# The last two row blocks of a gated mix as one: first feed-forward layer by seven quarter products

## Chip, cores and metric

The kernel runs on one core of a Trainium2 chip. The metric is device time in microseconds, as the median of several executions. The profile is one execution seen by the hardware profiler, with its own time. TensorE (PE) multiplies, VectorE (DVE) and GpSimd (POOL) do elementwise work, ScalarE (ACT) does copies and functions, and SyncE (SP) issues most DMAs.

## The reference

```python
x = A_x                                   # 1 x 2048 x 512, all float32
g = _sigmoid((x * gate_w).sum(-1, keepdims=True))
a = _A_ref(x, A_wqkv, A_w_phi, A_wo)      # linear attention, 32 heads of 16
b = _B_ref(x, B_w1, B_b1, B_w2)           # mish(x @ w1 + b1) @ w2, 512 -> 1376 -> 512
return g * a + (1 - g) * b
```

In the attention q and k go through a 16x16 matrix per head; the feature map of each is the softmax of the result beside the softmax of its negative. Then `kv = phi_k^T v`, `z` is the sum of `phi_k` over all rows, and the output is `(phi_q kv) / (phi_q z)`, times `wo`.

## The kernel before, in words

**Precision.** Each matmul operand is split in a high part (ScalarE's copy to fp32r) and a low part (VectorE or GpSimd: the value minus the high part). A product is three groups of matmuls: high by high, high by low, low by high. The moving side is 512 wide, so 128 of the contraction against 512 columns is one matmul; every matmul goes through the helper `mm` (L130), every ScalarE instruction through `act` (L157), so the profile tells them apart by tile names.

**Stages.** P fuses the 16x16 matrices into the weights of q and k. A0 to A7 take 256 rows of x each: they make q, k and v (tiles `proj`), write q to DRAM (`pqd`), and collect `kv` (tile `kvp`) and `z`. In A1 to A7, q and k come out of seven products of half operands instead of eight (steps `s1` to `s7`, with the sums `bc`, `ca`, `qa`). B0 to B3 take 512 rows each: the feed-forward layers, softmax of q, the numerator, the output projection, the gate and the output. W steps load and split w1, w2 and wo.

**A row block B.** The first layer has 11 units of 128 columns (`up0` to `up10`). `up` makes 12 matmuls, `w1` against `xbh` and `xbl`, in one bank; `mi` is Mish with the bias; `h` and `l` split the result; the second layer (`dn`, tile `down`) adds, for each of four row tiles a to d, three matmuls per unit into a bank of its own. Unit 0 holds the last 96 columns of the first 736 and the gate; its low part is packed in spare rows (`ha`, `hb`, `ph`, `pi`, `pc`), so it takes two matmuls per row tile and one short piece (`dc`). For attention, `lq` loads q, `mx`, `mn`, `d0`, `d1`, `E`, `S` make both softmaxes, `T`, `D`, `m`, `de`, `rd`, `sc`, `es` the denominator and scaling, `tr`, `st`, `ld` turn the features by way of DRAM (`eTd`, `eT`), `nu` is the numerator (32 short matmuls, tile `num`), `oh` and `ol` split it, `wo` is the output projection (12 matmuls). `ag`, `fi` and `so` scale it with the gate, add the second layer and store.

**Order.** Each engine runs its instructions in the order of the table `ORDER`. A line names a stage; a word is a step of it, and `B1:` ahead of a step means another stage. A step's last letter v or g says VectorE or GpSimd. `@` gives buffer or bank numbers; `^` makes a GpSimd step wait for the VectorE step written ahead of it. Words of different engines that stand side by side need not run at the same time.

**PSUM and SBUF.** Of eight banks three have the tag `a` (first layer, num, wo), four `dn` (second layer) and one `kv`. `w1` in both parts lies at a fixed place (the arena, 11264 floats per partition); x's two parts and the gather tiles lie in the pool.

Of the kernel before, what the change touches and what calls it, by code (L numbers as in the profile page):

```python
# [91 lines left out]
def tile_gated_mix(ctx: ExitStack, tc: tile.TileContext, xT, wv, wkT, wqT, bd, w1a, w1b, b1, w2a, w2b, wo, out):  # L92
# [29 lines left out]
    nc.alloc_sbuf_tensor("arena", [P, sum(FIXED.values())], F32)
    top = nc.sbuf_base
    for tag, n in list(FIXED.items()):
        top -= 4 * n
        for part, o in (("h", 0), ("l", 2 * n)):
            FIXED[tag + part] = {dt: nc.alloc_sbuf_tensor_at(tag + part + x, [P, n // 2], dt, offset=top + o) for dt, x in ((F32R, "r"), (F32, "f"))}

# [905 lines left out]
```

## Time and profile before

| | |
|---|---|
| median of 3 runs | 439.56 us (439.36 to 439.75) |
| profiled execution | 439.43 us |
| its span | 437.7 us, 7246 instructions |
| TensorE busy | 432.8 us, 2835 matmuls |
| VectorE, ScalarE, GpSimd busy | 319.9, 231.4, 182.3 us |
| DMA | 55.14 MB, mean 126 GB/s |
| chain that ended last | by line: proj 28%, up 28%, down 27%, wo 10%, num 2% |

In the profile an instruction's line ends with the number of instructions, then busy time and mean length, and behind the bar the idle time of its engine ahead of it with what ended it. A row of the chain is start, length and what ran. A matmul's own length overlaps with the next one's, so a run of matmuls is read by start and end of the whole piece.

### The profile page before, as it was taken

To read this page: it belongs to the slowest core of one execution; us is meant where nothing else is said; L and a number is where in the kernel's file an instruction comes from. 1 tells how busy PE (TensorE), PEld (TensorE's weight loads), DVE (VectorE), ACT (ScalarE), POOL (GpSimd) and SP (SyncE) were. 2 spreads that over 40 slices of the span, in tenths; PEclk is the share of its full clock that TensorE was granted. 3 is DMA by queue.
4 is the path that set the end of the run, shared out by engine and by line. 5 is a ranking of instruction groups with operands and counts; after the bars stand their busy time and mean duration, and the time that the engine had idled before them with its cause. 6 is when DMAs were issued, how large, how long until landed. Compare 5 with 4: busy or idle time off the path is not lost.

```text
span 437.7 us, 7246 instructions
## 1 busy us (share of the span) xinstructions
PE 432.8 (99%) x2835; PEld 352.0 (80%) x2835; DVE 319.9 (73%) x441; ACT 231.4 (53%) x317; POOL 182.3 (42%) x147
## 2 busy tenths in 40 slices
PE   8999999999999999999999999999999999999996
PEld 7888888888888888887878887878888778888775
DVE  3996799789988989998784896676776537557212
ACT  3775446538444958673633826638646166262321
POOL 4438748858568013565034452131442500631210
PEclk9999999999999999999999999999999999999999
DMA  7612284676982423463302244321614410034303
GB/s 272 234 73 75 119 191 117 171 172 153 262 233 89 143 77 96 145 214 120 114 12 96 96 155 160 120 74 54 211 49 168 135 35 25 24 108 173 121 32 120
DMA packets 30041, 55.14 MB, mean 126 GB/s; under 512 B 5364, under 2 KB 15348, under 8 KB 30008
## 3 DMA queue, kind: packets, MB, share of 16 engines
q1 hardware_dynamic: 27960, 48.26, 32.8%
q0 software_dynamic: 1904, 6.17, 7.4%
q8 instruction: 22, 0.36, 0.3%
q10 hardware_dynamic: 144, 0.26, 0.2%
q14 instruction: 11, 0.09, 0.1%
HBM read 32.26 MB, written 22.03 MB: 124 GB/s over the span
## 4 chain that ended last, share of the span: by engine, by line
PE 99%; DVE 0%; DVEq 0%; issue 0%
PE proj L130 28%; PE up L130 28%; PE down L130 27%; PE wo L130 10%; PE num L130 2%; PE kvp L130 2%; PE fuse L130 1%; PE warm L130 1%; PE z L130 0%; DVE io L886 0%; PE kvT L654 0%; DVEq L1030 0%; DVE ones L190 0%
## 5 line engine op out<-in xcount | busy, mean ns | idle before, releaser
L705 POOL TENSOR_TENSOR l<-act,h 128x512 fp32r<-128x512 f32 x28 | 37.7, 1346 | 117.9 <-ACT h L157 37.5
L157 ACT ACTIVATE act<-up,cst 128x512 f32<-128x512 f32 x44 | 30.1, 687 | 54.8 <-PE up L130 47.3
L157 ACT ACT_TABLE_LOAD x34 | 43.6, 1283 | 5.6 <-PE up L130 5.0
L317 DVE TENSOR_REDUCE Sm<-E 128x64 f32<-128x1024 f32 x32 | 38.7, 1208 | 6.6 <-ACT E L157 6.6
L130 PE MATMUL wo<-woh,ohl 128*128 128x512 f32 x128 | 41.4, 389 | 0.0
L157 ACT ACTIVATE h<-act 128x512 fp32r<-128x512 f32 (+1 forms) x48 | 30.0, 629 | 18.9 <-PE down L130 10.8
L130 PE MATMUL down<-w2ah,h 128*128 128x512 f32 x96 | 38.0, 396 | 0.0
L157 ACT ACTIVATE E<-E 128x1024 f32<-128x1024 f32 x32 | 33.4, 1056 | 8.4 <-DVE E L311 4.7
L130 PE MATMUL down<-w2al,h 128*128 128x512 f32 x96 | 37.4, 390 | 0.0
L130 PE MATMUL down<-w2bh,h 128*128 128x512 f32 (+1 forms) x81 | 31.5, 389 | 0.0
L130 PE MATMUL down<-w2bl,h 128*128 128x512 f32 (+1 forms) x81 | 31.3, 387 | 0.0
L130 PE MATMUL down<-w2bh,l 128*128 128x512 f32 (+1 forms) x81 | 31.3, 386 | 0.0
L130 PE MATMUL down<-w2ah,l 128*128 128x512 f32 x80 | 31.1, 389 | 0.0
L130 PEld LDWEIGHTS wo<-woh,ohl 128*128 128x128 f32 x128 | 24.0, 188 | 5.0
L836 DVE STREAM_TRANSPOSE E<-E 128x1024 f32<-128x1024 f32 x16 | 19.9, 1243 | 10.3 <-POOL E L333 10.0
L130 PE MATMUL up<-xbh,w1ahr 128*128 128x512 f32 x96 | 25.9, 392 | 0.0
L130 PE MATMUL up<-xbh,w1alr 128*128 128x512 f32 x96 | 25.7, 389 | 0.0
L130 PE MATMUL up<-xbl,w1ahr 128*128 128x512 f32 x96 | 25.7, 389 | 0.0
L886 DVE SCALAR_TENSOR_TENSOR io<-down,cst,io 128x512 f32<-128x512 f32 (+1 forms) x17 | 11.7, 705 | 18.7 <-ACT io L157 9.3
L130 PE MATMUL wo<-wol,ohl 128*128 128x512 f32 x64 | 24.9, 389 | 0.0
L130 PEld LDWEIGHTS down<-w2ah,h 128*128 128x128 f32 x96 | 18.0, 188 | 5.6 <-issue 1.2
L796 DVE TENSOR_REDUCE Dn<-T 128x64 f32<-128x1024 f32 x16 | 19.3, 1208 | 4.3 <-POOL T L792 4.0
(197 smaller groups left out, 1062.6 us busy)
## 6 DMA issues: line engine op xcount, KB each, us to landing
eTd<-E SPq DMA_DIRECT2D x16, 512.0 KB, 2.6
eT<-eTd SPq DMA_DIRECT2D x64, 128.0 KB, 2.7
xraw<-in_xT_dram SPq DMA_DIRECT2D x15, 512.0 KB, 4.1
zd<-E POOLq DMA_DIRECT2D x10, 512.0 KB, 5.4
pqd<-qs SPq DMA_DIRECT2D x16, 256.0 KB, 3.7
pq<-pqd SPq DMA_DIRECT2D x16, 256.0 KB, 2.9
out_dram<-io SPq DMA_DIRECT2D x10, 256.0 KB, 2.0
raw<-in_w2a_dram SPq DMA_DIRECT2D x3, 512.0 KB, 4.3
```

What stands on the lines that cost most here:

```text
L130: return pin(nc.tensor.matmul(*a, **k))
L157: return pin(A_.activation(out_, in_, fn, **k))
L317: pin(V.tensor_reduce(d["S"], hv(d["E"][:, :]), axis=AX.X, op=ALU.add))
L705: on_(e)(e.tensor_sub(U[i]["l"], U[i]["a"], f32(U[i]["h"])))
L796: pin(V.tensor_reduce(d["D"], hv(d["T"][:, :]), axis=AX.X, op=ALU.add))
L836: at(key, f"tr{t}", lambda d=d: pin(V.transpose(d["E"][:, :], d["E"][:, :])))
L886: pin(V.scalar_tensor_tensor(io[t][:, sl], dn[t][:, sl], og_sb[:, i % 8 : i % 8 + 1], io[t][:, sl], op0=ALU.mult, op1=ALU.add))
```

## The change

B2 and B3 become one block of 1024 rows, S1 (B0 and B1 stay). Its first layer is computed in pairs of units. With x in four quarters (512 rows by half of the 512 features) and the weights of two units in four quarters (half of the features by 128 columns), a pair takes seven products of a quarter by a quarter instead of eight, six matmuls each:

- x's quarters and their sums, eight operands in high and low parts, lie over `w1`'s place and x's old place, once B1 is done with them. Quarters are loaded anew from DRAM (`x11` and so on, 18 DMAs of 256 KB), and five sums (`t3`, `t2`, `t1`, `ta`, `t4`) are made.
- Weights are loaded anew for each pair (`la`, `lb`: 6 DMAs, 1 MB) and summed (`sa`: two, `sb`: three operations of 128x256), then split (`wah`, `wal`, `wbh`, `wbl`).
- A pair's products: `s1` opens a bank, `bc` copies it to a second bank, `s2` ends the first; `s7` goes to the `kv` bank, which `cm` copies out; `s6` and `s5` go on in the second bank; `ca` adds the second bank and `cm`'s copy into a third, `s4` ends that; `qa` updates the copy, `s3` ends the second bank. `ma` to `md` are Mish for two units and two row halves.
- Activations of the second row half go to DRAM and come back (`sp`, `al`, ten units of 256 KB each way), and their second layer (`en`) comes after that of the first half.
- The single unit's split weights are stored and loaded again for the second half (`wst`, `wl_1`).
- The gathers of S1 all use the one tile `eT`; `tt` is the place of the pair's weights.
- `ORDER` is new from its first line on, for all stages.

The diff, cut to its core:

```diff
-SLOTS = "01201010213"
+SLOTS = "01201010123"
 ORDER = """
-    P0| lk0 fk0@01 lx0@0 xh0 xl0g kh01 kl01 lk2 fk2@23 kh00 p0a0@0 kl00 p0a1@1 p0b1 lx1 xh1 lk1 xl1g^ fk1 kh11 kh10 lk3 fk3 kl10 lx2 xh2 kh21 lq3 kl11 p0c1 kl21 p1a1
+    P0| lk0 lx0@0 xh0 lx2 fk0@01 kh00 xh2 kh01 p0a0@0 kl00 kl01 p0a1@1 lk1 xl0g^ fk1 kr00 kr01 xl2v p0b0 p0c0 lq0 kh10 lq1 kh11 kl11 fq0@23 lx1 xh1 xl1g fq1 qh01 kl10
...
+    B1| S1:XL11g dn9c es3v tr3 mi10@1 h10@3 S1:d01v@2 S1:T0v@0 S1:d11v S1:E1 st3 S1:xt1 mi4@0 h4@5 S1:mx2@1 l4g^@4 dn9ad S1:D0@1 ol0 wo0 wo1@0 dn1b S1:S1@1 S1:la0
+    S1| sa0g^ B0:so1 B1:ag0@1 B1:dn1d B1:ld2 B1:ld3 B1:nu1@1 B1:oh1@01 T1v@1 B1:dc D1@0 B1:dn4b m1 de1 B1:l10g@0 B1:dn10d t1v mn2@1 XL21v B1:dn10a d12g@0 x22 lq4@1 XHt1
+    S1| B1:ol1 B1:wo2 XH22 XHt3 B0:so3 B1:wo3@2 XL22v B1:dn4d xt4 XLt1v d02g lb0@0 sb0v B1:h3@6 B1:l3v@7 B1:dn3da E2 T2v@0 wah0 B1:dn10c wal0v XHt2 XLt2v wl_0@0 wh_0@1
+    S1| wo_0v tag^ wst B1:ag2@3 B1:ag3@2 B1:fi3 B1:so3 B1:dn3c B1:dn4c B1:fi2 u0@1 mu0@1 gr0@0 gs0 B1:so2 hb0@2 s10@2 B1:dn4a mx4@0 ha0@5 B1:dn3b bc0@1 t4v B1:dn10b s20
+    S1| XLt3v XHt4 s70 s60 la1 XLt4g^ ph0 pi0 dn0c@2 ma0@4 dn0a@0 h01@6 S0@0 dn0b@3 m0 B1:fi0 B1:ag1@2 de0 B1:fi1 cm0@7 ca0@2 l01g@3 dn1b wbh0@3 wbl0g s40 rd0 sc0 sa1g
+    S1| s50 lb1@0 dn1d@1 mb0@0 rd1 sc1 pc0 dn0d h02@4 wah1 qa0 md0 s30 l02v@1 dn2b wal1v B1:so0 sb1g^ es1v sp2 tr1 mc0@5 sp1 dn1c st1 ge0 gg0 s11@0 bc1@2 s71 s61 wbh1@3
...
+    S1| sc5 dn9cad mn6@1 d16v@3 md3 dn9b cm4@7 ca4@2 s44 mb4@2 mx6@1 h010@5 sp8 d06v al4@0 dn8d al1@6 s54 l010v@3 dn10ba m4 h12@2 dn10cd wo3@0 l12g^@5 qa4 md4 sp10 wo2
...
-    FIXED = {"w1a": NFA * 1024, "w1b": NFB * 1024}
...
+    AREA = 17408
...
+    for tag, o, *sizes in ((("w1a", 0, NFA * 512, NFA * 512), ("w1b", NFA * 1024, NFB * 512, NFB * 512), ("xbh", 11264, 2048), ("xbl", 13312, 2048), ("tt", 15360, 2048), ("wa", 15360, 1024, 1024),
+                            ("wb", 14336, 512, 512)) + tuple((f"xo{i}", 2048 * i, 1024, 1024) for i in range(7))):
+        fixed(tag, o, *sizes)
...
+    XTAG = {"11": 0, "21": 1, "t3": 2, "t2": 3, "t1": 4, "22": 5, "t4": 6, "12": 4}
+    PAIRS = ((0, 1), (2, 3), (4, 6), (7, 8), (9, 10))
...
+            def prod(bank, n, b, o, start, stop):
+                m = 0
+                for wi, xi in ((0, 0), (1, 0), (0, 1)):
+                    for k in range(2):
+                        c, t = b * 256 + k * P, wv_(n, wi)
+                        if (n, b) == ("b", 2):
+                            c, t = wi * 256 + k * P, w["c"]
+                        mm(ps[bank], t[:, c : c + P], xv(o, xi)[:, k, :], start=(start and m == 0), stop=(stop and m == 5), skip_group_check=True)
+                        m += 1
...
+            def bc():
+                ps["q0"] = psum("up", "a")
+                act(ps["q0"], ps["k0"])
+
+            def ca():
+                ps["k1"] = psum("up", "a")
+                pin(V.tensor_add(ps["k1"], ps["q0"], U[1, j]["a"]))
+
+            def cm():
+                U[1, j] = {"a": k2("act", "hl")}
+                act(U[1, j]["a"], ps["m7"])
+
+            def qa():
+                pin(V.tensor_add(U[1, j]["a"], ps["q0"], U[1, j]["a"]))
...
+            at(key, f"s2{p}", lambda: prod("k0", "a", 1, "21", False, True))
+            at(key, f"s6{p}", lambda: prod("q0", "a", 3, "t2", False, False))
...
+            at(key, f"s5{p}", lambda: prod("q0", "b", 1, "t1", False, False))
+            at(key, f"s4{p}", lambda: prod("k1", "b", 0, "t4", False, True))
...
+            at(key, f"s3{p}", lambda: prod("q0", "b", 2, "22", False, True))
...
-    for b in range(NB):
+    for b in range(2):
         b_ops(b)
+    sb_ops(1)
```

The remaining steps of S1 (softmax, numerator, output projection, gate, output, second layer) do for 1024 rows what B2 and B3 did for 512 each.

More of the change, by code (lines that the diff above doesn't have):

```diff
@@ L119, in tile_gated_mix, with fixed @@
     ENG = (("v", V), ("g", G_))
-    FIXED = {"w1a": NFA * 1024, "w1b": NFB * 1024}
[L122 to L127, printed above, removed]
+    FIXED = {}
+    AREA = 17408
+    nc.alloc_sbuf_tensor("arena", [P, AREA], F32)
+    base = nc.sbuf_base - 4 * AREA
+    def fixed(tag, o, *sizes):
+        n = sum(sizes)
+        for part, q, size in [("", 0, n)] + [(p, i * sizes[0], m) for i, (p, m) in enumerate(zip("hl", sizes)) if len(sizes) > 1]:
+            FIXED[tag + part] = {dt: nc.alloc_sbuf_tensor_at(tag + part + x, [P, size], dt, offset=base + 4 * (o + q)) for dt, x in ((F32R, "r"), (F32, "f"))}
+    for tag, o, *sizes in ((("w1a", 0, NFA * 512, NFA * 512), ("w1b", NFA * 1024, NFB * 512, NFB * 512), ("xbh", 11264, 2048), ("xbl", 13312, 2048), ("tt", 15360, 2048), ("wa", 15360, 1024, 1024),
+                            ("wb", 14336, 512, 512)) + tuple((f"xo{i}", 2048 * i, 1024, 1024) for i in range(7))):
+        fixed(tag, o, *sizes)
     def mm(*a, **k):
@@ L308, in dd @@
             E = hv(d["E"][:, a * 512 : (a + 1) * 512])
-            note = on_(e) if key[0] == "B" else pin
+            note = on_(e) if key[0] in "BS" else pin
             if (a == 0) != negative:
@@ L321, in feat_ops @@
         for a in range(2):
-            if key[0] == "B":
+            if key[0] in "BS":
                 for x, e in ENG:
@@ L710, in down_mm @@
                 dn[t] = psum("down", "dn")
-            if part[1] == 512:
-                left[t] -= 1
-            sl = slice(*part)
-            mm(dn[t][:, sl], a, w[:, sl], start=(n == 3 * NF), stop=(n == 1), skip_group_check=True)
+            left[t] -= 1
+            mm(dn[t], a, w, start=(n == 3 * NF), stop=(n == 1), skip_group_check=True)
         def down(i, t):
-            parts = ((0, 512),)
-            if b == NB - 1 and len(left) == 4 and sum(left.values()) == 3:
-                ends.append(t)
-                parts = ((0, 256), (256, 512))
-            for part in parts:
-                for a, x in (("h", 0), ("h", 1), ("l", 0)) if i else (("h", 0), ("i", 1)):
-                    down_mm(t, U[i][a][:, t * P : (t + 1) * P], w2_tile(UNITS[i], x), part)
-        ends = []
-        def cols(t):
-            return (slice(0, 256), slice(256, 512)) if t in ends else (slice(None),)
+            for a, x in (("h", 0), ("h", 1), ("l", 0)) if i else (("h", 0), ("i", 1)):
+                down_mm(t, U[i][a][:, t * P : (t + 1) * P], w2_tile(UNITS[i], x))
         def ha(x):
@@ L896, in b_ops, with save, rows @@
         x_ops(b)
+    XTAG = {"11": 0, "21": 1, "t3": 2, "t2": 3, "t1": 4, "22": 5, "t4": 6, "12": 4}
+    PAIRS = ((0, 1), (2, 3), (4, 6), (7, 8), (9, 10))
+    actd, wsplit = {}, {}
+    def save(k, parts):
+        n = parts[0].shape[1]
+        wsplit[k] = tc.dram_tile([P * len(parts), n], F32, name=f"ws{k}")
+        for j, t in enumerate(parts):
+            pin(Sy.dma_start(wsplit[k][j * P : (j + 1) * P, :], f32(t)))
+    def rows(c):
+        return slice((c % 2) * SC, (c % 2) * SC + SC)
```

419 lines of the change are left out of this document (370 added, 49 removed).

## The prediction

> **What bounds the kernel now.** I read the page first, then TensorE's waits, then the chain of waits that ended last, then the groups of instructions, the stretches of the last two row blocks, and the timeline of VectorE and GpSimd beside each other. The page:
>
> ```profile
> span 437.7 us, 7246 instructions
> ...
> PE 432.8 (99%) x2835; PEld 352.0 (80%) x2835; DVE 319.9 (73%) x441; ACT 231.4 (53%) x317; POOL 182.3 (42%) x147
> ...
> PEclk9999999999999999999999999999999999999999
> ...
> PE 99%; DVE 0%; DVEq 0%; issue 0%
> ```
>
> TensorE is busy 99% of the span, at the full granted clock, and it alone is the chain. TensorE's waits have one line, ahead of the first matmul:
>
> ```profile
> PE warm L130 <- DVE ones L190: 1.1, 1, 1.1
> ```
>
> A busy TensorE can still be waiting inside, since ends are modelled, so I look at its pace. The chain, in order of time:
>
> ```profile
> 5.38 1.60 PE fuse L130 x64
> ...
> 7.05 1.19 PE proj L130 x3
> 8.25 1.09 PE fuse L130 x64
> 9.34 6.36 PE proj L130 x27
> ...
> 282.44 2.72 PE up L130 x12
> ...
> 331.78 10.20 PE down L130 x45
> ...
> 345.38 1.02 PE num L130 x32
> ...
> 434.02 0.03 issue
> 434.05 0.48 DVE io L886
> ```
>
> Twelve up matmuls take 2.72 us and 45 down matmuls 10.20 us: 227 ns each, in both rows. The start is looser: 30 proj matmuls at that pace are 6.80 us and took 7.55, and the first 64 fuse matmuls took 0.51 us longer than the second 64. So about 1.3 us of waiting sits at the start and almost none behind it. The matmuls end at 434.05; 3.65 us of eviction, output and end follow. The profiled execution took 439.43 us (1.73 around the span), 0.13 under the median of 439.56.
>
> **TensorE's share of the change.** Now the first layer of two blocks is 2 x 11 units x 12 matmuls = 264. Afterwards ten units go in five pairs, each seven quarter products of 6 matmuls, and the eleventh stays at 12 per block: 5 x 7 x 6 + 24 = 234. Second layer, attention, output projection, and the final matmuls in halves keep their numbers. So 30 matmuls go. The price of one is not the mean in its group,
>
> ```profile
> L130 PE MATMUL up<-xbh,w1ahr 128*128 128x512 f32 x96 | 25.9, 392 | 0.0
> ```
>
> since 392 ns is how long one is in the array while the next already runs (that would give 11.8 us); it is the pace: 30 x 227 ns = **6.80 us**. On the other side nothing is added for TensorE to do, so with no new wait the profiled time is 439.43 - 6.80 = 432.6 us. Whatever else the change costs, it costs as waits in a TensorE queue that today has none.
>
> **What the other engines get.** Rows for the pieces:
>
> ```profile
> L157 ACT ACT_TABLE_LOAD x34 | 43.6, 1283 | 5.6 <-PE up L130 5.0
> L157 ACT ACTIVATE act<-up,cst 128x512 f32<-128x512 f32 x44 | 30.1, 687 | 54.8 <-PE up L130 47.3 <-PE down L130 6.4 <-DVE l L705 0.8
> L157 ACT ACTIVATE h<-act 128x512 fp32r<-128x512 f32 x40 | 25.2, 630 | 18.8 <-PE down L130 10.8 <-POOL l L705 5.6 <-DVE lc L741 1.1
> L157 ACT ACTIVATE xbh<-xraw 128x1024 fp32r<-128x1024 f32 x8 | 8.3, 1053 | 3.8 <-PE up L130 3.3 <-DMA xraw<-in_xT_dram 0.4
> ...
> L157 ACT ACTIVATE wkh<-fuse 128x256 fp32r<-128x256 f32 x2 | 0.8, 383 | 5.7 <-PE fuse L130 5.7
> ```
>
> ```profile
> L420 DVE TENSOR_TENSOR proj<-proj,qs 128x512 f32<-128x512 f32 x7 | 4.9, 697 | 1.4 <-ACT qs L157 0.8 <-PE proj L130 0.5
> ...
> L552 DVE TENSOR_TENSOR w2al<-raw,w2ah 128x1024 fp32r<-128x1024 f32 x2 | 2.4, 1210 | 0.0
> ...
> L382 DVE TENSOR_TENSOR w1blr<-sraw,w2bl 128x512 fp32r<-128x512 f32 x3 | 2.1, 687 | 0.1
> L376 DVE TENSOR_TENSOR sraw<-xraw,sraw 128x256 f32<-128x256 f32 x4 | 1.7, 422 | 0.1
> ```
>
> ```profile
> L705 POOL TENSOR_TENSOR l<-act,h 128x512 fp32r<-128x512 f32 x28 | 37.7, 1346 | 117.9 <-ACT h L157 37.5 <-DVE h L741 26.3 <-PE down L130 24.8
> ...
> L376 POOL TENSOR_TENSOR sraw<-xraw,sraw 128x256 f32<-128x256 f32 x10 | 7.6, 763 | 0.4
> ...
> L552 POOL TENSOR_TENSOR w2al<-raw,w2ah 128x1024 fp32r<-128x1024 f32 x1 | 2.4, 2402 | 4.7 <-DVE w1alr L552 4.7
> ```
>
> - ScalarE: x's high parts go from four of 128x1024 to eight (+4.2 us); per pair the weights' high parts (1053 + 630 + 383) and two copies of a bank (about 0.63 each): 3.3 us, five times 16.6; 0.6 for the single unit. Together 21.4 us. Counted in the written order, the changes between Exp and Mish go from 35 to 33, so table loads stay.
> - VectorE: two additions into a bank or tile per pair (10 x 0.70), x's sums and low parts by the order's suffix (+4 net of 128x1024, 4.8), weights' sums (6 + 3 of 128x256, 3.8), low parts (5 x 1.21 and 0.69): 22.4 us.
> - GpSimd: +5 net of 128x1024 (12.0), weights' sums (4 + 12 of 128x256, 12.2), low parts of the second half (5 x 2.11): 34.8 us.
>
> The stretches from the first matmuls of block B2 to the last matmul, with TensorE, weight loads, VectorE, ScalarE, GpSimd, clock, DMA share and GB/s:
>
> ```profile
> 0.00:20.00 20.00, 18.76 (x314) 15.75 (x315) 12.15 (x24) 12.10 (x22) 9.83 (x17) 1.00 0.71 252
> 230.50:282.50 52.00, 52.00 (x257) 42.45 (x256) 36.56 (x52) 27.76 (x34) 17.91 (x13) 1.00 0.38 132
> 282.50:354.00 71.50, 71.50 (x371) 57.48 (x370) 46.63 (x68) 39.92 (x51) 25.32 (x17) 1.00 0.33 111
> 354.00:434.00 80.00, 80.00 (x440) 63.95 (x438) 38.95 (x60) 31.78 (x45) 17.37 (x11) 1.00 0.22 76
> ```
>
> In these 203.5 us VectorE is busy 122, ScalarE 99 and GpSimd 61. With the additions, and every other step on the engine it has now: 145, 121 and 95. (The new order moves some steps between VectorE and GpSimd; their sum, 240 of 407 us, is what I hold to.) No engine is full on average. DMA gets 14.3 MB more (x's quarters 2.6, weights 5.2, the single unit's weights 1.3, ten activations out and back 5.2), 70 GB/s over these stretches, on 76 to 132; the first 20 us moved 252. SP's queue gets some 65 issues. The price of a fetch of 256 KB, from issue to landing, has this row:
>
> ```profile
> pq<-pqd SPq DMA_DIRECT2D x16, 256.0 KB, 2.9
> ```
>
> With ScalarE's copy and GpSimd's difference a fetched unit is ready 2.9 + 0.63 + 1.35 = 4.9 us after its issue. For seven of the ten fetches the order has 2 to 21 us of TensorE's work between fetch and first use; units 3, 5 and 9 are fetched right ahead of it, and are hidden only if SP gets there early, as it does now for B3's last gather, which stands right ahead of its num matmuls. SP waits for the fetch's buffer, and behind it stand x's last quarter, output stores and the attention gathers, for which the last single unit and the num matmuls wait. I take nothing for these; one of the three exposed would give up to 4.9 us, 439.0 in all.
>
> **Where it can pinch.** The start is reordered too: I count its 1.3 us as unchanged, between all of it gone and twice it. At the end nothing changes in kind. The opening of the merged block is the dense place, and here a resource counts that the page has no column for. VectorE and GpSimd beside each other:
>
> ```profile
> 186.74 1.28 POOL L705 TENSOR_TENSOR l<-act,h 128x512 fp32r<-128x512 f32 x1 [1.36 <-ACT h L157]
> ```
>
> ```profile
> 186.90 1.17 DVE L808 TENSOR_TENSOR Dn<-Dn 128x32 f32<-128x32 f32 x1
> ...
> 206.60 0.19 DVE L808 TENSOR_TENSOR Dn<-Dn 128x32 f32<-128x32 f32 x1
> ```
>
> VectorE's small addition at 186.90 took 1.17 us; the same operation at 206.60, with GpSimd idle, took 0.19. The slow one ended at 188.07, just behind GpSimd's 188.02: it had waited for GpSimd's operation. So operations with two SBUF inputs on these two engines go one at a time. Count both engines' from B1's ninth unit to the first product of the second pair. TensorE has 32 x 3 + 4 x 2 down matmuls, eight products, four output projections, two units of the plain first layer, two sets of num matmuls and one short piece: 53.3 us. VectorE has 15 of 128x1024 (18.2), nine half as wide (6.2), three of 128x256 (1.3) and ten small ones (0.2 each): 27.7. GpSimd has 5 of 128x1024 (12.0), ten half as wide (13.5) and eight of a quarter (6.1): 31.6. Together 59.3, that is 6.0 more than TensorE's work. The 11.8 us ahead of it hold 8.3, so 3.5 can be done early; and about 3.5 of the 6.0 (a weight sum, a scaling) is not needed by that product. So the wait is between 0 and 2.5 us; I take 1.0. If all 6.0 came through, the time would be 438.6.
>
> The hand-offs inside a pair are the other place: a bank is copied between its first and second product, a sum is made in a fresh bank, and a tile is updated before the last product. An addition takes 0.70 us. The least work between its producer and its user in the written order is 1.13 us (five matmuls, pair 0, ahead of its last product) and 1.36 (six, pairs 1, 3 and 4). So 0.4 to 0.6 us is left for semaphores and for whatever VectorE has ahead; behind the waiting addition stand softmax steps and the next addition. One VectorE operation too many (0.69 to 1.21) costs 0.1 to 0.8. I take 0.5 for all five pairs.
>
> Sum: 439.43 - 6.80 + 1.0 + 0.5 = **434.1 us**.
>
> **The rivals.**
> 1. *The shared ports bind the opening.* For it: the 59.3 against 53.3. Against it: VectorE's and GpSimd's steps can run early. All 6.0 paid, with the 0.5: 439.1; half: 436.1. The Trainium skill's page "SBUF — State Buffer", section "Who interferes with whom", says that these engines share one port pair as an exclusive lock, held for a whole instruction; the row at 186.90 agrees.
> 2. *Every pair waits (slower).* The sum's bank can be the one that Mish is still reading. If ScalarE is in Exp then, the product waits for a table load, Mish and the addition: 1.28 + 0.69 + 0.70 = 2.7 us, five times 13.4, giving 446.0. It decides at 1.6 us per pair, (440.4 - 432.6) / 5. Against it: between the bank's last product and its next use lie 4.8 us or more of other matmuls in the three pairs that reuse it at once.
> 3. *Data late at the opening.* Behind B1's last up matmul SP issues x's quarters (1.05 MB) and weights (0.52) ahead of the second half's gathers (1.05), and these feed the num matmuls. At 252 GB/s they take 10.4 us; TensorE has 10.9 us (eight down groups and two output projections) until then. With the 2.9 us from issue to landing on top they are 2.4 us late: 0 to 2.4 us more than the forecast, to 436.5. By the Trainium skill's "TensorE: Matmul & The Clock Gate", "Part 1", a wait over about 3.4 us would also halve the clock for a while; no row here shows such a wait.
> 4. *The change does not deliver:* the order of all stages is new, and a few tenths in each of ten places give back the 6.8. Nothing in the profile speaks for it but that there is no slack: 439 to 440.
>
> **How the numbers follow.** Forecast 0.62 (432.6 to 435.6), rival 1 0.15 (435.6 to 439.1), rival 3 0.10 (434.1 to 436.5), rival 2 0.09, rival 4 0.04. A measurement of this kernel can tell 0.2%, 0.88 us, from no change. Faster: all of the forecast and rival 3, most of rival 1: 0.84. Same: the rest of rival 1 and most of rival 4: 0.06. Slower: 0.10. The range runs from 431.8 (the start's waits mostly gone, nothing new) to 438.4 (rival 1 nearly paid).
>
> **What would show it.** Right: up matmuls down by 30 at 227 ns, TensorE busy near 426 us, the chain all TensorE, VectorE and GpSimd together near 559 us busy (502 now). The 1.0 shows as gaps or over-long pieces in TensorE's chain between B1's last unit and the second pair; the 0.5 as pieces of products above 1.36 us each. Rival 1: VectorE operations far above 1.21 us there; rival 2: a gap ahead of the same product in each pair; rival 3: TensorE's num waiting for the eT gather. The forecast is wrong if the span is over 436.7 or the pace is no longer 227 ns.

## The result, and the profile after

The changed kernel is **slower** by 0.75%: 442.87 us (median of 4 runs, 442.06 to 444.07) against 439.65 us for the kernel before in the same session (439.36 to 439.93), ratio 1.0075 with a 95% interval of 1.0046 to 1.0105. The prediction was 434.1 us, 431.8 to 438.4. The profiled execution took 442.13 us, 1.73 around a span of 440.4, so the span grew by 2.7 us. Medians, ranges and ratios here and below are of fast runs; one slow run, of e4's kernel (447.55 us), is left out. The page after:

```profile
span 440.4 us, 7480 instructions
...
PE 428.7 (97%) x2805; PEld 345.8 (79%) x2805; DVE 359.7 (82%) x476; ACT 249.2 (57%) x345; POOL 213.4 (48%) x173
...
PE 67%; DVE 19%; DMA 6%; issue 3%; ACT 2%; SPq 1%; POOL 1%; DVEq 0%; POOLq 0%; ACTq 0%
```

The 30 matmuls are gone (2805 for 2835) and VectorE and GpSimd have 573 us of work together (559 forecast). But the chain, all TensorE before, is TensorE for only 67%. TensorE's waits, which had one line before (us in total, times, longest; three lines of 0.2 us are left out):

```profile
PE kvp L139 <- DVE E L342: 1.8, 1, 1.8
PE warm L139 <- DVE ones L199: 1.1, 1, 1.1
PE num L139 <- issue: 1.0, 1, 1.0
PE fuse L139 <- issue: 0.7, 1, 0.7
PE proj L139 <- DVE xbhr L1402: 0.7, 1, 0.7
PE wo L139 <- DVE ohl L857: 0.6, 1, 0.6
PE fuse L139 <- DMA bds<-in_bd_dram: 0.5, 1, 0.5
PE proj L139 <- DVE proj L429: 0.5, 1, 0.5
PE down L139 <- POOL l L1065: 0.4, 1, 0.4
```

Look at the tile names: `fuse`, `proj` and `kvp` belong to the opening phase and the A stages, which the change was not about; `wo` is B0's output projection at 212 us, `num` B1's numerator at 280. Only the last line is the merged block. The stretches say the same (TensorE, weight loads, VectorE, ScalarE, GpSimd busy, clock, DMA share, GB/s):

```profile
0.00:20.00 20.00, 16.75 (x303) 13.29 (x304) 9.33 (x18) 12.09 (x22) 8.70 (x19) 1.00 0.73 251
20.00:180.00 160.00, 157.74 (x1169) 130.08 (x1168) 143.53 (x186) 89.23 (x128) 96.18 (x75) 1.00 0.51 140
180.00:260.00 80.00, 79.24 (x406) 63.56 (x405) 77.14 (x106) 45.20 (x58) 28.78 (x17) 1.00 0.45 146
260.00:300.00 40.00, 38.82 (x225) 30.42 (x224) 29.59 (x34) 29.17 (x36) 20.66 (x12) 1.00 0.60 190
300.00:437.00 137.00, 136.12 (x710) 108.43 (x708) 99.46 (x136) 73.55 (x105) 59.13 (x50) 1.00 0.52 164
```

In the kernel before TensorE was busy for 18.76 us of the first stretch and then without a break to its last matmul. Here it loses 2.0, 2.3, 0.8, 1.2 and 0.9 us; the last is the merged block.

Busy time hides short waits, so I also took, from the trace's matmul records, the time from each matmul's start to the next one's less the pace of its kind (227 ns for 512 columns), and summed it by the same stretches. The change in the total has to be the change in the span plus the 6.8 us of matmuls that went, and it is: 9.5 = 2.7 + 6.8.

| TensorE beyond its pace, us | 0–20 | 20–180 | 180–260 | 260–300 | 300–end | sum |
|---|---|---|---|---|---|---|
| before | 1.50 | 1.32 | 0.35 | 0.36 | 0.45 | 3.98 |
| after | 4.15 | 3.64 | 1.74 | 2.20 | 1.78 | 13.51 |
| more | 2.65 | 2.32 | 1.39 | 1.84 | 1.33 | 9.53 |
| e3: before's code, new order ahead | 4.79 | 4.65 | 0.69 | 0.36 | 0.49 | 10.98 |
| e4: after, gathers first | 6.35 | 4.08 | 1.85 | 0.36 | 1.14 | 13.78 |
| e6: after, old order into B0, gathers first | 1.47 | 1.28 | 9.75 | 0.39 | 2.04 | 14.93 |
| e15: after, old order into A7, gathers first | 1.92 | 3.27 | 0.85 | 0.47 | 0.83 | 7.33 |
| e16: as e15, gathers late | 1.76 | 2.96 | 1.60 | 2.11 | 0.88 | 9.31 |
| e17: as e15, one step more moved | 1.76 | 2.94 | 1.80 | 0.45 | 2.44 | 9.39 |
| e18: after, one scaling earlier | 4.23 | 2.61 | 1.83 | 1.97 | 1.02 | 11.66 |

Each row is one execution. So two thirds of the loss (2.65 + 2.32 + 1.39 = 6.4 of 9.5) stand ahead of the merged block, 1.8 at its opening, 1.3 in it.

**Two waits up close.** The chain at the largest, in the last A stage (start, length, what ran):

```profile
150.03 1.35 DVE h L738
151.38 0.01 issue
151.39 2.80 DVE h L738
154.20 0.02 issue
154.22 0.56 DVE Sm L339
154.78 0.02 issue
154.80 1.39 DVE E L342
156.20 0.14 issue
156.33 0.65 PE kvp L139 x32
```

TensorE waits for VectorE's scaling (L342). Ahead of it stand two packing steps of B0 (L738), which took 4.16 us; GpSimd beside them:

```profile
148.42 5.22 POOL L496 TENSOR_TENSOR zacc<-zacc,E 128x1024 f32<-128x1024 f32 x2 [7.50 <-ACT h L166]
```

Two additions, ending at 150.83 and 153.64; the two packing steps end at 151.38 and 154.19, each 0.55 us behind one. In the kernel before one such packing step took 0.69 us with GpSimd idle:

```profile
153.01 0.69 DVE L741 TENSOR_TENSOR h<-act,h 32x512 fp32r<-32x512 f32 x1
```

This is the sharing that the prediction priced for the merged block's opening, at a place where it was not looked for. The Trainium skill's page "SBUF — State Buffer", section "Who interferes with whom", has these two engines lock a shared port pair for a whole instruction; these rows agree.

The other, at the opening:

```profile
275.62 3.69 DMA eT<-eTd
279.31 0.14 issue
279.45 0.59 PE num L139 x2
280.04 1.01 issue
281.05 1.09 PE num L139 x30
```

The first two num matmuls wait for a gather that took 3.69 us. The third starts after 1.01 us that the view calls "issue", waiting for nothing it shows. The last of the eight gathers was issued at 276.07 us, and the slowest of them took 4.9 us, which ends at 281.0; experiment e4 shows that this too was a gather. Between 266 and 284 us the eight gathers took a median of 3.9 us from issue to landing (2.7 over the whole of the kernel before):

```profile
eT<-eTd SPq DMA_DIRECT2D x8, 128.0 KB, 3.9
```

### The profile page after: what moved, and what is told of

The parts are those of the page before. It is cut to its first block, busy times and chain, and to the rows that moved or that the text cites. A ratio compares the mean times of both kernels' runs of the same rounds, so it can differ in the third digit from the quotient of the medians.

```text
span 440.4 us, 7480 instructions
## 1 busy us (share of the span) xinstructions
PE 428.7 (97%) x2805; PEld 345.8 (79%) x2805; DVE 359.7 (82%) x476; ACT 249.2 (57%) x345; POOL 213.4 (48%) x173
## 4 chain that ended last, share of the span: by engine, by line
PE 67%; DVE 19%; DMA 6%; issue 3%; ACT 2%; SPq 1%; POOL 1%; DVEq 0%; POOLq 0%; ACTq 0%
PE proj L139 21%; PE down L139 19%; PE up L139 17%; PE wo L139 6%; DVE E L342 3%; DVE Sm L326 3%; DVE Dn L793 2%; PE num L139 2%; DMA eT<-eTd 1%; DVE T L789 1%; DMA zd<-E 1%; DVE E L833 1%; DMA bds<-in_bd_dram 1%; DVE h L738 1%; DVE E L320 1%
## 5 line engine op out<-in xcount | busy, mean ns | idle before, releaser
L714 POOL TENSOR_TENSOR l<-act,h 128x512 fp32r<-128x512 f32 x17 | 24.6, 1446 | 54.7 <-PE down L139 44.7
L166 ACT ACTIVATE act<-up,cst 128x512 f32<-128x512 f32 x39 | 26.7, 688 | 33.6 <-PE up L139 27.3
L1065 POOL TENSOR_TENSOR l<-act,h 128x512 fp32r<-128x512 f32 x17 | 22.1, 1301 | 46.9 <-ACT h L166 34.8
L342 DVE TENSOR_TENSOR E<-E,Dn 128x1024 f32<-128x1024 f32 x16 | 23.4, 1462 | 0.3
L166 ACT ACTIVATE io<-wo,cst 128x512 f32<-128x512 f32 x16 | 10.7, 684 | 22.5 <-PE wo L139 22.5
L139 PEld LDWEIGHTS down<-w2al,h 128*128 128x128 f32 x96 | 18.0, 188 | 3.6
L139 PEld LDWEIGHTS down<-w2bh,h 128*128 128x128 f32 x81 | 15.2, 188 | 4.2 <-issue 1.2
L166 ACT ACTIVATE v<-proj 128x512 f32<-128x512 f32 x16 | 9.4, 594 | 15.7 <-PE proj L139 9.8
```

What stands on the lines that cost most here:

```text
L139: return pin(nc.tensor.matmul(*a, **k))
L166: return pin(A_.activation(out_, in_, fn, **k))
L342: on_(eng)(eng.tensor_mul(hv(d["E"][:, :]), hv(d["E"][:, :]), d[by][:, :, None].to_broadcast([P, 2 * H, DH])))
L714: on_(e)(e.tensor_sub(U[i]["l"], U[i]["a"], f32(U[i]["h"])))
L1065: on_(e)(e.tensor_sub(U[r, i]["l"], U[r, i]["a"], f32(U[r, i]["h"])))
```

## The experiments

**Theory 1:** the loss is in the written order ahead of the merged block (start, A stages, first two row blocks) and in a gather queued behind the merged block's loads; the merged block itself gives what it was costed at. **Theory 2:** the loss belongs to the merged block and its opening, and would be there under any order ahead. (Where the expectations say 2.7 us for the A stages and 1.0 for B0 and B1, the table has 2.3 and 1.4.) Most kernels have the changed kernel's code and a table `ORDER` whose first part is that of the kernel before. The joint of the two is the difficulty: by then one order has done steps that the other would do later, and has left others undone.

A table holds more than a sequence. Of the steps with a letter v or g ahead of the merged block 55 change between VectorE and GpSimd, and buffer numbers change too; a part taken from a table brings these along. Where "order" stands below it means all of this. Against the changed kernel only e4 and e18 change the sequence alone.

**e1, old order to the end of B0.** The joint, at `st3`, in the new table:

```diff
+    B0| d03v E3 B1:XL0v B1:XL1v B1:up0@2 B1:mi0@7 dc st1 ld1 nu0@0 oh0@01 B1:lq2@0 B1:ha@3 sc2 es2v B1:mn0@0 tr2 st2 ld2 WL0g^ S3@0 ol0 T3g^@0 D3@1 m3 B1:up2@1
+    B1| mi2@1 gr@1 B0:de3 B0:rd3 B0:sc3 B0:es3v B0:tr3 B0:st3 mn2@1 B0:dn6c B0:dn10b mx2@1 d02v@1 d12v d10g^@2 E2 lq3@0 B0:dn10a B0:gg0 B0:wo1@0 mn3@1 d13v@3
```

> The changed kernel with the old written order for P, A0 to A7 and B0, up to the store of B0's last features; from there on the new order, with the merged block. Theory 1: the merged block by itself gains, and the new order of the stages ahead of it loses about as much as it gains. In the changed kernel's trace TensorE lost 2.65 us more than before in the first 20 us, 0.7 around 70 us, 2.0 at 156 us and 0.9 around 213 us; all of these should go: 442.9 - 6.2 = 436.7 us, a ratio to the kernel before of 0.993. Theory 2: the merged block brings the waits on itself (fixed places of x and the gather tile, longer program, more DMAs), the order only shows them: 441 to 443. Theory 3 (rival 1 of the prediction, shared ports at the opening): nothing changes, 442 to 443.

Measured: 449.0 us, ratio 1.0224 (1.0206 to 1.0241). Missed. The waits ahead are gone (1.91 us at the start, 1.34 in the A stages), but the joint made one of 8.8:

```profile
PE up L146 <- ACT io L173: 8.8, 1, 8.8
```

`gr@1` now waits for a buffer that the new order frees late, with ScalarE's queue behind it. Inconclusive as a time.

**e2, old order for the first 104 steps.**

```diff
+    P0| ql01 qr00 qh00 ql00 W:t1v W:h0 W:t3v A0:d01@1 qh10 ql10 A0:d10 A1:v1@2 W:t4g ql11 W:t2 W:h3 W:l0v W:l3v A1:v0@0 A1:ve0@3 A1:bc@1 A1:s2 A0:ldx@1
```

> The changed kernel with the old written order for the first 104 steps alone (stage P and the first steps of A0 and A1). Theory 1: the first 20 us lose 1.5 us instead of 4.15, the rest stays: 440.2 us, about the kernel before (1.001). If the new start is forced by what comes behind it (a wait that only moves), 442 to 443.

Measured: 447.59 us, 1.0187 (1.0163 to 1.0210). The start's waits fell to 1.77 us; the joint cost 4.7 us between 20 and 60, and near 283 us a late gather cost 3.8, most of it in slow matmuls behind the wait. Inconclusive as a time.

**e3, the reverse:** the code of the kernel before, unmerged, with the changed order through P, A and B0.

```diff
-SLOTS = "01201010213"
+SLOTS = "01201010123"
...
+    B0| tr3 st3 B1:up0@0 B1:mi0@1 B1:ha@4 es2v tr2 st2 gg0 WL1v dc nu0@2 B1:up2@1 oh0@01 ld2 ol0 dn6a B1:mi2@2 B1:gr@1 ld3 B1:mx0@1 B1:pc B1:gs wo1@2 ag1@3
```

> The kernel before, with B2 and B3 as they were, but with the new written order for P, A and B0 up to B0's second output projection; then the old order. Theory 1: it pays for the new order and has no merged block to gain from: 439.6 + 5 to 6 = 445 us, ratio 1.012 to 1.015. Theory 2: the order alone costs nothing: 439 to 440.

Measured: 446.1 us, 1.0145 (1.0127 to 1.0163). Theory 1 holds for P, the A stages and B0: with no merged block the new order alone costs 6.5 us. Its joint costs next to nothing (0.69 us in 180–260, 0.36 and 0.49 behind), and the waits are the changed kernel's own:

```profile
PE kvp L137 <- DVE E L340: 1.7, 1, 1.7
PE fuse L137 <- issue: 1.4, 1, 1.4
PE warm L137 <- DVE ones L197: 1.1, 1, 1.1
PE proj L137 <- DVE wkh L971: 0.7, 1, 0.7
PE proj L137 <- DVE proj L427: 0.6, 1, 0.6
PE fuse L137 <- DMA bds<-in_bd_dram: 0.6, 1, 0.6
```

**e4, gathers first:** the changed kernel with `ld2` and `ld3` of B1 ahead of the merged block's last quarter of x and first weights.

```diff
+    S1| d01v@2 T0v@0 d11v E1 B1:st3 B1:ld2 B1:ld3 xt1 B1:mi4@0 B1:h4@5 mx2@1 B1:l4g^@4 B1:dn9a B1:dn9d D0@1 B1:ol0 B1:wo0 B1:wo1@0 B1:dn1b S1@1 la0 sa0g^
```

> The changed kernel with one move: B1's second gather (eight DMAs of 128 KB) is issued ahead of x's first late quarters and the first pair's weights instead of behind them. If the 1.7 us that TensorE loses ahead of and inside B1's second num matmuls are DMAs queued behind 1.5 MB of the merged block's loads (rival 3 of the prediction), they go: 441.2 us, 0.996 of the changed kernel. If the gap belongs to instruction supply, as its label in the trace (issue) could mean, it stays: 442 to 444. The moved loads may come late in their turn at the first pair, then the gain is less.

Measured: 442.1 us (440.77 to 443.69), 1.0057 (1.0043 to 1.0071). Between 260 and 300 us TensorE is back at 0.36 us beyond pace, as in the kernel before, from 2.20; so the 1.01 us of "issue" was a gather too. The time shows it only in part: this profiled execution lost 6.35 us at the start, where the same steps lost 4.15 in the changed kernel's. Its matmuls ran at half pace there: a full granted clock is first recorded at 14.2 us, in every other trace between 4.5 and 7.3, and until then the first 512-column matmul of a group took 0.56 to 0.59 us instead of 0.31 to 0.34. The new start differs from execution to execution (4.79 us in e3's, 4.23 in e18's), and e4's runs spread by 2.9 us (0.8 for the kernel before beside them).

**e5 and e6, the joint inside B0** (e6 with the gathers first).

```diff
+    B0| lq3@0 W:O11g^ rd0 sc0 dn6a es0v tr0 T1v@1 h10@2 l10g^@6 dn10c D1@1 st0 B1:LX1@1 S1@0 m1 B1:lq0@1 de1 rd1 sc1 es1v tr1 ld0 mn3@1 d13v@3 B1:XH1 mx3@1
+    B0| d03g B1:lq2@0 B1:mn2@0 E3 dn6c WL0g T3v@0 dn10b st1 B1:XL0g B1:mx2@1 ld1 B1:d02v@1 S3@0 D3@1 m3 B1:d12v B1:XL1v de3 rd3 sc3 sc2 B1:mn0@1 B1:d10g^@2
```

> The changed kernel's code with the merged block, but with the written order of the kernel before through the opening phase, the A stages and the first half of the first row block, and the changed kernel's order from there on; the same work is done. Unlike the earlier joint at the end of the first row block, nothing that ScalarE queues here has to wait long for a tile of VectorE. Theory 1 (the loss is in the re-planned order ahead of the merged block: about 2.7 us at the start, 2.7 in the A stages, 1.0 in the first two row blocks): about 436.7 us, ratio to the kernel before 0.993, with TensorE's waits beyond pace at the start near 1.5 us as in the kernel before and none near 156 us. Theory 2 (the loss belongs to the merged block and its opening, whatever the order ahead of it): 441 us or more, ratio 1.003 or more.

> As the run before it, and the two last gathers of the second row block are issued ahead of the last quarter of x and of the first weights of the merged block on their queues. Theory 1 with the gather as the opening's loss: about 434.9 us, ratio 0.989, with the numerator matmuls of the second row block no longer waiting near 280 us. If the opening waits for something else (shared ports, splits of x): the same as the run before it, about 436.7 us. Theory 2 (the loss belongs to the merged block): 441 us or more.

Measured: 444.74 us, 1.0137 (1.0110 to 1.0164), and 444.04, 1.0100 (1.0085 to 1.0115). Missed, again by one wait at the joint, 6.0 us at 209, with slow matmuls behind it: VectorE stands before `mn2` until a gather has landed, and x's low parts queue behind. The gathers first take 1.1 us out of the opening (1.46 to 0.39 in e6).

**e7 and e8, the joint later in B1 and at its start** (both with the gathers first).

```diff
+    B0| dn10a B1:d00g B1:E0 wo0 ag0@1 fi0 B1:up7@2 B1:h2@2 dn6c B1:l2v@6 B1:dn2a@1 B1:dn2d@2 B1:mi1@1 nu1@0 B1:mn2@1 B1:mx2@1 B1:d02v@2 B1:d12v B1:E2 B1:lq3@0
...
+    B0| de3 rd3 sc3 es3v tr3 st3 B1:mn2@1 dn6c dn10b B1:mx2@1 B1:d02v@1 B1:d12v B1:d10g^@2 B1:E2 B1:lq3@0 dn10a gg0 wo1@0 B1:mi2@1 B1:mn3@1 B1:d13v@3 B1:mx3@0
```

> The changed kernel's code; the order of the kernel before through the opening, the A stages, the first row block and the first 60 steps of the second (so the joint lies where ScalarE's gate row and VectorE's differences around it stand as in the kernel before), the changed kernel's order from there on, and the two last gathers of the second row block ahead of the merged block's loads. Theory 1 (the loss is in the order ahead of the merged block and in the late gather, and the merged block gives what it was costed at): 434 to 436 us if the joint itself costs under 2 us, ratio 0.987 to 0.992. Theory 2 (the loss belongs to the merged block): 441 us or more with no single wait at the joint that accounts for it.

> As the run before it, with the joint some 28 steps earlier and the gate row and one Mish of the second row block left to the changed kernel's order. Theory 1: 434 to 437 us if the joint costs under 3 us; what is above it should stand as one wait near 200 to 225 us and nowhere else. Theory 2: 441 us or more without such a wait.

Measured: 448.36 us, 1.0196 (1.0166 to 1.0225), with waits of 5.2, 3.1 and 1.5 us at the joint; and 441.68, 1.0052 (1.0035 to 1.0069), with two, 2.5 and 2.1.

**e9 and e10, that joint mended twice.**

```diff
-    B0| ag1@3 wo0 B1:ph B1:pc B1:mx0@1 B1:d03v B1:E3 B1:d00v B1:E0 B1:T3v@1 ag0@1 fi0 B1:gr@0 B1:up5@1 B1:mi5@5 B1:hb@0 ld3 B1:up1@0 B1:mi1@4 B1:pi B1:up7@2
+    B1| mx3@0 B0:ag1@3 B0:wo0 ph pc mx0@1 d03v gr@0 E3 d00v E0 T3v@1 B0:ag0@1 B0:fi0 up5@1 mi5@5 hb@0 B0:ld3 up1@0 mi1@4 pi up7@2 dn0d@2 h5@7 lq1@1 B0:nu1@1
...
+    B1| mi2@1 B0:de3 B0:rd3 B0:sc3 B0:es3v B0:tr3 B0:st3 mn2@1 B0:dn6c B0:dn10b mx2@1 d02v@1 d12v d10g^@2 E2 gr@0 gs mx0@1 d00v E0 lq3@1 B0:dn10a B0:gg0
```

> The run before it (order of the kernel before up to the end of the first row block, the changed kernel's order behind it, two gathers ahead) with the two waits at its joint taken away: ScalarE does one Mish and the gate row of the second row block ahead of the exponentials for which it waited, instead of behind them. Theory 1 (the merged block and its opening give what they were costed at, and the changed kernel's loss is in the order ahead of it): the joint's 2.2 and 2.7 us of waiting and the slow matmuls behind them, together about 6.9 us, go; 434.5 us, ratio 0.988. Theory 2 (the loss belongs to the merged block): the time stays at 441 us, the waiting coming back elsewhere behind 280 us.

> Same kernel as the run before it, with the joint written out anew for 33 steps: the gate row of the second row block is taken before its last gather of q and uses the other buffer, so that the gather does not wait, and ScalarE does the Mish and copies on which TensorE waited ahead of the last exponential. Nothing else is changed. Theory 1: the 7.4 us beyond pace between 220 and 240 us fall to about 1, and with everything else as it was the time is 435.5 us or less, ratio 0.991. Theory 2 (the loss belongs to the merged block): 441 us or more, the waiting coming back behind 280 us.

Measured: 443.24 us, 1.0101 (1.0063 to 1.0139), and 446.90, 1.0167 (1.0153 to 1.0181). Both missed: each step moved ahead left another late (in e10 a wait of 4.6 us for `ohl`). At this joint moving single steps gained nothing.

**e11 and e12, the joint at the end of the A stages**, where the sets of steps done in the two orders differ least.

```diff
+    A6| s3 qe0@1 sh1 sl1v kk A7:m7@0 A7:s6 A7:ca@2 st0 mx1@0 B0:LX1@0 A7:E0 d00 E0 v1@1 A7:S0@1 A7:rS0 B0:XH0 B0:XL0g B0:XH1 A7:v0@0 A7:ve0@1 W:L3@1 d01@1
...
+    B0| gs mi0@4 hb@7 ha@0 A7:qe0@0 A6:ml0v A7:st0 A7:ve0@1 W:L3@0 W:H3 A6:ve1@2 A6:S1@0 lq0@0 W:O5v A7:ve1@3 up5@1 up1@2 mi1@2 A7:ml0g A6:rS1 A6:ml1v A6:z0v
+    A6| z1g A7:z0g^ B0:mn0@1 B0:d10g^@0 A7:S1@1 B0:mi5@1 B0:h5@3 B0:l5g^@5 B0:pi B0:lq3@0 B0:ph A7:rS1 A7:ml1v B0:mx0@0 B0:d00v B0:up4@0 B0:h1@6 A7:z1v
```

> The changed kernel's code; the order of the kernel before through the opening and the A stages up to the end of the sixth (where the sets of steps done in the two orders differ by ten steps, the fewest of any place), the changed kernel's order from there on, with the two last gathers of the second row block ahead. Theory 1 with its parts (2.65 us at the start and 2.7 us in the A stages come from the order there): 442.9 - 2.65 - 2.7 - 1.1 (gather) = about 436.5 us, ratio 0.993, if the joint costs nothing; each us at the joint adds one. Theory 2 (the loss belongs to the merged block): 441 us or more with no waiting at the joint.

> As the run before it, with the joint 32 steps later, in the last A stage and at the opening of the first row block. Theory 1: about 436.5 us, ratio 0.993, if the joint costs nothing. Theory 2: 441 us or more with no waiting at the joint.

Measured: 445.96 us, 1.0134 (1.0081 to 1.0187), with waits of 3.2 and 2.0 us at the joint; 443.53, 1.0092 (1.0075 to 1.0108), with 4.2 and 1.4. In e12 all else is quiet.

**e13 and e14, that joint mended:** `S1` and `rS1` of A7 go ahead of B0's `mn0`, and `W:H3` back by five steps; e14 also moves both `kv` behind two more units.

```diff
-    A6| z1g A7:z0g^ B0:mn0@1 B0:d10g^@0 A7:S1@1 B0:mi5@1 B0:h5@3 B0:l5g^@5 B0:pi B0:lq3@0 B0:ph A7:rS1 A7:ml1v B0:mx0@0 B0:d00v B0:up4@0 B0:h1@6 A7:z1v
+    A6| z1g A7:z0g^ A7:S1@1 A7:rS1 B0:mn0@1 B0:d10g^@0 B0:mi5@1 B0:h5@3 B0:l5g^@5 B0:pi B0:lq3@0 B0:ph A7:ml1v B0:mx0@0 B0:d00v B0:up4@0 B0:h1@6 A7:z1v
...
-    A7| zh1@10 B0:l1v@1 A6:kv zl1v kv B0:up2@2 B0:mx2@1 B0:up3@1 B0:dn1d@3 zh0 zl0g z0b@1 zc0 W:O3v B0:dn1a@0 km@0 z1b@2 zc1 B0:mi3@2 B0:d02g@1 B0:dn0a
+    A7| zh1@10 B0:l1v@1 zl1v B0:up2@2 B0:mx2@1 B0:up3@1 A6:kv kv B0:dn1d@3 zh0 zl0g z0b@1 zc0 W:O3v B0:dn1a@0 km@0 z1b@2 zc1 B0:mi3@2 B0:d02g@1 B0:dn0a
```

> The run with the joint in the last A stage, with the two waits at that joint taken away: VectorE's sum and scaling of the last A stage stand ahead of its reduction that waits for a gather (instead of behind it), and ScalarE's split of one piece of the weights, which waits for a load, stands behind the values' eviction. All else is as it was. Theory 1 (the changed kernel's loss is in the order ahead of the merged block, 2.65 us at the start and 2.7 us in the A stages, and in the late gather, 1.1): the 7.2 us beyond pace between 140 and 160 us fall to about 1, and the time is 435 to 437 us, ratio 0.990 to 0.994. Theory 2 (the loss belongs to the merged block): 441 us or more, the waiting coming back behind 280 us.

> As the run before it, and the last two groups of matmuls of the A stages stand behind two more units of the first layer on TensorE, 5.4 us later. Theory 1: 435 to 437 us; if the values are late at the joint, this one is the faster of the two by what is left of that wait. Theory 2: 441 us or more.

Measured: 443.90 us, 1.0107 (1.0089 to 1.0126), and 444.93, 1.0113 (1.0097 to 1.0130). Both missed. I had moved the wrong step: the scaling for which TensorE waits is `ml1`, not `rS1` (that is the reciprocal). e13 has a single wait left in the whole trace beside the start, and what it costs can be read off:

```profile
156.67 1.08 PE L146 MATMUL kvp<-E,v 128*32 128x64 f32 x32 [5.30 <-DVE E L349]
157.68 2.08 PE L146 MATMUL up<-xbhr,w1ahr 128*128 128x512 f32 x4
159.55 1.91 PE L146 MATMUL up<-xbhr,w1alr 128*128 128x512 f32 x4
161.26 1.50 PE L146 MATMUL up<-xblr,w1ahr 128*128 128x512 f32 x4
162.59 1.08 PE L146 MATMUL up<-xbhr,w1ahr 128*128 128x512 f32 x4
```

**e15 and e16, `ml1` moved too** (e16 with the gathers where the changed kernel has them).

```diff
-    A6| z1g A7:z0g^ A7:S1@1 A7:rS1 B0:mn0@1 B0:d10g^@0 B0:mi5@1 B0:h5@3 B0:l5g^@5 B0:pi B0:lq3@0 B0:ph A7:ml1v B0:mx0@0 B0:d00v B0:up4@0 B0:h1@6 A7:z1v
+    A6| z1g A7:z0g^ A7:S1@1 A7:rS1 A7:ml1v B0:mn0@1 B0:d10g^@0 B0:mi5@1 B0:h5@3 B0:l5g^@5 B0:pi B0:lq3@0 B0:ph B0:mx0@0 B0:d00v B0:up4@0 B0:h1@6 A7:z1v
```

> As the run with the mended joint in the last A stage; there VectorE's scaling of the last A stage's exponentials, on which the last group of that stage's matmuls waited 5.3 us, still stood behind a reduction that waits for a gather. Now it stands ahead of it. Nothing else differs. Theory 1 (the changed kernel's loss is in the order ahead of the merged block and in the late gather; the merged block gives what it was costed at): the one wait left in that trace and the slow matmuls behind it go, about 7 us: 434.5 to 436 us, ratio 0.988 to 0.992. Theory 2 (the loss belongs to the merged block): 441 us or more.

> The same kernel, with the two last gathers of the second row block where the changed kernel has them, behind the merged block's last quarter of x and first weights on the queues. Theory 1 with the gather as a part: 1.1 to 1.8 us above the run beside it, the numerator matmuls waiting near 280 us. If the gather is hidden: the same time as the run beside it.

Measured: e15 **437.90 us** (436.80 to 439.47), ratio 0.9962 (0.9950 to 0.9975): faster than the kernel before, and 5.0 us under the changed kernel, whose merged block it has. That is 1.9 above the range expected; the joint still costs 2 us in 20–180, and the profiled execution is the fastest of eight (436.80). e16: 440.47, 1.0025 (1.0013 to 1.0038); the late gathers cost 2.6 us in the medians and 2.0 us of span in the profiled executions (436.2 against 434.2; e16's too is its fastest), 1.6 of it in the opening. Theory 2 is out. From 240 us on e15 has one wait in the view:

```profile
PE up L146 <- issue: 0.2, 1, 0.2
```

and TensorE is full at the opening, with VectorE and GpSimd busy for 69 us together in these 53 us:

```profile
245.00:298.00 53.00, 53.00 (x290) 42.33 (x289) 43.78 (x52) 35.15 (x45) 25.16 (x16) 1.00 0.60 194
```

**e17, `z1` moved too.**

```diff
-    A6| z1g A7:z0g^ A7:S1@1 A7:rS1 A7:ml1v B0:mn0@1 B0:d10g^@0 B0:mi5@1 B0:h5@3 B0:l5g^@5 B0:pi B0:lq3@0 B0:ph B0:mx0@0 B0:d00v B0:up4@0 B0:h1@6 A7:z1v
+    A6| z1g A7:z0g^ A7:S1@1 A7:rS1 A7:ml1v A7:z1v B0:mn0@1 B0:d10g^@0 B0:mi5@1 B0:h5@3 B0:l5g^@5 B0:pi B0:lq3@0 B0:ph B0:mx0@0 B0:d00v B0:up4@0 B0:h1@6
```

> The kernel with the clean joint and the early gathers, and one more step at the joint: VectorE adds up the last A stage's sums of exponentials ahead of its reduction that waits for a gather, so that the two matmuls that spread those sums (at 160 us) no longer wait 0.8 us for GpSimd's split of them. Theory 1: 1 to 1.5 us below the run with the clean joint: about 436.6 us, ratio 0.993, faster than the kernel before and than the changed kernel. If that wait only moves to the next hand-off: 437.9 us as without it.

Measured: 437.89 us (437.08 to 438.28), 0.9954 (0.9941 to 0.9968). The wait of 0.8 us moved to the next hand-off (0.86 at 168 us), as the second expectation had it. e15 and e17 beat both kernels, by the same amount.

**e18, the changed kernel with `rS1` and `ml1` ahead of B0's packing.**

```diff
-    A7| ml0g A6:rS1 A6:ml1v A6:z0v A6:z1g z0g^ B0:mn0@0 B0:d10g^@0 S1@0 B0:mi5@2 B0:h5@4 B0:l5g^@6 B0:hb@7 B0:pi B0:lq3@1 B0:ph rS1 ml1v B0:mx0@0 B0:d00v
+    A7| ml0g A6:rS1 A6:ml1v A6:z0v A6:z1g z0g^ B0:mn0@0 B0:d10g^@0 S1@0 B0:mi5@2 B0:h5@4 B0:l5g^@6 B0:hb@7 rS1 ml1v B0:pi B0:lq3@1 B0:ph B0:mx0@0 B0:d00v
```

> The changed kernel with one edit: in the last A stage VectorE's scaling of the exponentials, on which TensorE waits 1.8 us at 156 us, stands ahead of two small packing steps of the first row block. In the changed kernel's trace those two steps took 4.16 us instead of 1.38, ending just behind GpSimd's two additions that ran beside them. If that is the cause: the scaling waits for at most one of GpSimd's additions, the wait at 156 us goes, and the time falls by its 2.0 us to about 440.9 us, ratio 1.003. If the scaling itself is held up as long, or the packing steps' users wait instead: the same time as the changed kernel, 442.9 us, ratio 1.0075.

Measured: the wait at 156 us is gone, and with it the 2.0 us beyond pace between 150 and 160; 0.8 us of them came back elsewhere between 140 and 180. The packing steps still take 4.24 us beside GpSimd's operations, but nobody waits for them:

```profile
151.11 1.29 DVE L350 TENSOR_TENSOR E<-E,Sm 128x1024 f32<-128x1024 f32 x1
152.43 4.24 DVE L746 TENSOR_TENSOR h<-act,h 32x512 fp32r<-32x512 f32 x2
```

The profiled execution fell by 1.8 us, to 440.29, but by the table only 1.0 of it lies in 20–180; most of the rest (0.8) is in the merged block, which the edit doesn't touch (a fetch near 410 us came in time; see below). The median, 442.28 us (440.29 to 443.11), 1.0062 (1.0048 to 1.0076), is only 0.6 under the changed kernel's, with intervals that overlap: the trace shows what made the wait, the medians can't tell the gain from the spread.

## Why the prediction was wrong, step by step

- **TensorE's share, -6.80 us: right.** 30 matmuls fewer at the same pace, and the sum of matmul time and waits closes to 0.1 us. In e15 the span is 3.5 us under the kernel before: 6.8 less 3.35 of waits beyond the kernel before's. ("Almost none behind it" was a little too good: the table has 2.5 us behind the start in the kernel before.)
- **"The start is reordered too: I count its 1.3 us as unchanged": this step failed**, and with it the same silence on the A stages, B0 and B1, where the new order was counted at nothing. They cost 2.65, 2.32 and 1.39 us, 6.4 together, nearly all that was to be gained. The forecast allowed the start up to 1.3 us more; it took twice that. e3 has 3.3 us more at the start and 3.3 in the A stages without a merged block; e6 has the merged block, and the old order there, without either. For B0 and B1 no run is that clean: e15, e16 and e17 keep the changed kernel's order there and stand 0.5, 1.25 and 1.45 us above the kernel before. Rival 4 named the mechanism ("the order of all stages is new, and a few tenths in each of ten places give back the 6.8"), but at 439 to 440 us and a chance of 0.04 it was mis-sized: besides tenths, the wait at 156 us took 2.0 and the start 2.65. Its next sentence had the reason, "that there is no slack", and gave it too little weight: with TensorE 99% of the chain, a step that comes late in a new order has little to hide behind.
- **The opening's shared ports, +1.0: 0.1.** With the gathers out of the way (e4, e6, e15, e17) the opening stands at 0.36 to 0.47 us beyond pace, against 0.36 before. The count was off: it put 59.3 us of operations that go one at a time into the stretch. In e15's 53 us VectorE's operations with both inputs in SBUF were busy for 25.7 us and GpSimd's for 25.2, what they waited for each other included, and together they cover 44.4 us. So the other work ran earlier or later, and no run shows the rule itself to be too strict. The mechanism is real, and it came at 156 us.
- **Rival 3, data late at the opening (0 to 2.4 us): right, at 1.8.** e16 against e15 and e5 against e6 show it: 1.6 and 1.1 us in the opening. It belonged in the sum, and lay inside the range given.
- **The hand-offs, +0.5: right at the pairs.** One gap of 0.38 us ahead of a pair's product at 343; the chain's product pieces are near 1.36 us per six.
- **The fetches right ahead of their use, put at nothing: 0.7 in the changed kernel.** The prediction named units 3, 5 and 9 and took nothing for them. Unit 5's fetch was late (SyncE, ScalarE, GpSimd):

```profile
403.94 0.38 SPq L1013 DMA_DIRECT2D act<-actd  x1
...
408.88 0.63 ACT L166 ACTIVATE h<-act 128x512 fp32r<-128x512 f32 x1 [2.82 <-DMA act<-actd]
...
409.59 1.28 POOL L1065 TENSOR_TENSOR l<-act,h 128x512 fp32r<-128x512 f32 x1 [6.36 <-ACT h L166]
```

ScalarE's copy starts 4.9 us after the issue, where the prediction had 2.9, and TensorE waits for GpSimd's low part, the last line of its waits above. Of the 18 traces with the merged block seven have ScalarE waiting 2.65 us or more for this fetch (the changed kernel, e5, e6, e7, e9, e11, e17), and in these TensorE waited behind it; in the other eleven it was 2.1 us or less, and TensorE had no wait. All in all the merged block costs 0.4 (e15) to 2.5 us (e9) more than before behind 300 us.
- **Rival 2, every pair waits: didn't occur.** A single product waited for its sum in e2, e7, e9 and e10, by 0.3 to 0.9 us.

With its own terms and the measured prices the sum comes out: 439.43 - 6.80 + 6.4 (order ahead) + 1.8 (gather) + 1.3 (merged block) = 442.1 us, the profiled execution's 442.13. It is the measurement read back, not a second forecast.

Open: why the start costs what it does (first load, VectorE's splits and "issue" share 2.65 us, and it varies between runs, with half pace in two of the four profiled executions that have the new start, e4's and e18's, and in none of the sixteen with the old) was not taken apart, nor how much of the new order's cost is the sequence and how much the change of engines. Nor was why e15's and e17's executions have 1.9 to 2.6 us around their spans where both kernels have 1.7, which takes some 0.6 us of their gain.

## What to carry to other kernels

When a change comes with a new order for all stages, cost the order first: compare, step by step, what each engine's queue holds ahead of the operations that the bounding engine waits for, also in stages that the change does not touch. If the bounding engine has next to no waits today, a new order can hardly remove any and can add many. And a gather that feeds the bounding engine goes ahead of bulk loads on its queue, even if those are wanted soon.
